# Exchanging the order in which ScalarE and VectorE read the first two finished PSUM banks of a pair

## The chip, the core and the metric

One core of a Trainium2 chip runs the whole program. The metric is device microseconds (us) of one launch. The engines are TensorE (PE in the profile, with its weight loads as PEld), VectorE (DVE), ScalarE (ACT), GpSimd (POOL) and SyncE (SP, which issues transfers).

## The reference

Attention within chunks of 64 tokens makes `x`, and a two-layer network with softplus between the layers makes the output. All data is fp32.

```python
scores = scale * q_c @ k_c.T                 # 8 batches x 8 heads x 9 chunks of 64 x 64, head size 64
attn = exp(scores - max) / (sum + 1e-09)
x = (attn @ v_c) as 4608 tokens x 512
h = x @ w_in                                 # w_in 512 x 2048
g = max(h, 0) + log1p(exp(-abs(h)))          # softplus
out = g @ w_out                              # w_out 2048 x 512
```

## The kernel before

**Tiling.** The 4608 tokens are nine blocks of 512 (`MT`). Each operand of a matmul is split into a high and a low fp32r image, and three matmuls (high by high, low by high, high by low) make one product. Blocks 0 to 2 are computed plainly: first layer (line 635), softplus on ScalarE (line 652), second layer (line 1002). Blocks 3 to 8 are computed in three "supers" of two blocks each (blocks 3 and 4, 5 and 6, 7 and 8). A super runs over eight "pairs", and a pair is two neighbouring column blocks of `w_in`. Pairs are named by super and number, `0_0` to `2_7`, 24 in all.

**A pair.** Its first layer is a 2x2 block product made of seven products of sums (as in Strassen's and Winograd's schemes) instead of eight. They accumulate in four PSUM banks, and two bank pairs are allocated as two tiles named `pa`, from a pool of two (lines 778 to 789). Tile A holds banks 1 and 2, tile B holds banks 0 and 3. TensorE computes P1 (bank 1), P2 (bank 2), P0 (bank 0), P3 (bank 3), then P4 on top of bank 1, P5 on top of bank 2 and P6 on top of bank 0. With P5 the banks of tile A are final, and the next pair's P1 needs tile A to have been read to the end.

What ScalarE, VectorE and GpSimd do with the banks:

- `hold` (lines 791 and 792, ScalarE) copies banks 0, 1 and 2 after P0, P1 and P2 into SBUF (`wib` in the profile, from the tile `wib3`).
- `mix` (lines 794 to 805) makes six sums. `d` and `c22` read SBUF alone and run on GpSimd. `e` reads bank 3, `f` adds bank 1 to `d`, `f2` subtracts bank 2 from `f` in place, and `c11` adds bank 0 to that; these four run on VectorE. In the profile `f` is the group `wib<-pa,wib` of line 805; `e`, `f2` and `c11` are `wib<-wib,pa`.
- `soft` (lines 811 to 817, ScalarE) makes the four softplus blocks of the pair: `soft10` of bank 1, `soft01` of bank 2, `soft11` of the result of `c22`, `soft00` of the result of `c11`. In the profile these are `ends<-pa` and `ends<-wib` of line 816 in supers 0 and 1, and `qe<-pa`, `eT<-pa`, `wo_hi<-pa` and the like of line 814 in super 2 (`BOTH`), whose results stay in SBUF.
- `sp_hi` and `sp_lo` split the softplus blocks into images (`g_hi` on ScalarE, `g_lo` on VectorE: lines 656 and 660, in super 2 lines 918 and 922).

The four steps that read tile A when it is final are `soft10`, `soft01`, `f` and `f2`. `soft10` and `f` read bank 1, `soft01` and `f2` read bank 2.

**What else runs there.** In supers 0 and 1, `soft01` and `soft11` write a tile that `spill_store` (line 820, SP) sends to memory, and `soft01` of the next pair waits until it has landed. In between the pairs lie "bursts" of attention for later blocks. They use `pa` tiles, VectorE transposes (line 544, `eT<-qe`) and ScalarE's exp (line 583). The exp needs another activation table, so the first softplus behind a burst has an `ACT_TABLE_LOAD` ahead of it. In super 2 the second layer is also computed with sums of products (lines 895, 922 and 938), and GpSimd and ScalarE prepare its weights (lines 863 to 881).

**What sets the order.** All work is written down as tasks with an engine, a cost, an urgency (`urg`) and the tasks that it needs (`Plan`, lines 34 to 157). A list scheduler goes through simulated time, gives each free engine the most urgent task that is ready by its own cost figures, and emits the instructions in that order. The tile framework then adds the semaphore waits, by tile and not by bank. A task that is ready later in the simulated time can therefore fall behind other tasks of its engine, and each engine runs its instructions in the order in which they were emitted. TensorE's own order is fixed ahead of that by hand-written lists. The pair's tasks are added in lines 1417 to 1480.

Of the kernel before, what the change touches and what calls it, by code (L numbers as in the profile page):

```python
# [160 lines left out]
def chunked_attention_softplus_ffn(  # L161
# [972 lines left out]
    def due(g):  # L1134
        if isinstance(g, tuple):
            n, second, j = g
            if n in BOTH:
                return D0 + SUPER * n + (98 + 1.36 * j if second else 12.2 * j + 9)
            return D0 + SUPER * n + (8 * PAIR + 2.6 * j if second else PAIR * j + 9)
        return T0 + TG * g  # L1140

    def tag(at):
        return "_".join(map(str, at)) if isinstance(at, tuple) else at
# [4 lines left out]
    for u, (g, is_in, fc) in enumerate(units):  # L1148
        (of_in if is_in else of_out)[fc] = u
        d = due(g) - 4  # L1150
# [30 lines left out]
    for i in range(FIRST_BLK):  # L1181
        d, kw = ATT_AT[i], KS
# [115 lines left out]
    for key, (pv, ps) in bursts.items():  # L1298
        d, at = due(key), tag(key)
        for n in range(2):  # L1300
            needs, rel = [], []
            if pv is not None:
                i = 2 * pv + n
# [12 lines left out]
            if ps is not None:  # L1316
                i = 2 * ps + n
# [21 lines left out]
        for n in range(2):  # L1339
            i = a + n  # L1340
# [24 lines left out]
    for j in range(FC // 2):  # L1365
        d = due(FC + 3 * j)
# [23 lines left out]
    for n, m in enumerate(SUPERS):  # L1390
        d = due((n, 0, 0)) - X_URG
        x_in = [f"xh{TPM * m + t}" for t in range(2 * TPM)]
        for k in range(7):
# [6 lines left out]
            needs = x_in + gone  # L1400
            if k in X_SUMS:
# [8 lines left out]
                needs = [f"xs{n}_{k}"] + gone  # L1410
            if k == 1:
                needs = needs + [f"xH{n}_0"]
# [4 lines left out]
    for at, w in enumerate(pairs):  # L1417
        n, j, name = w["s"], w["j"], w["name"]
        d = due((n, 0, j)) - 9
        for part in range(2):  # L1420
            needs = [] if at > 1 else [f"G1_{FAST * FC - 1}"]
            if not at and not part:
                needs = [f"B{BURST_AT[-1]}_{i}" for i in range(2)]
            if n == 0:
                needs += [f"wd{j}_{i}" for i in range(3)] + own
            if n in BOTH and j % 2:
                needs += [f"x{q}{n}_{k}" for q in "HL" for k in range(7)]
            plan.add(f"ring{part}_{name}", QUEUE["ring"], ISSUE[QUEUE["ring"]], partial(ring_load, w, part), needs, urg=d - 20, kb=660 if part else 880,
                     take=[(("ring", "other")[n in BOTH and j % 2] + str(part), [f"P{6 if part else 3}_{name}"])] if at or part else [],
                     after=[f"ring{part}_{pairs[at - 1]['name']}"] if at else [])  # L1430
        for k in range(7):
            needs = [f"ring{k // NX}_{name}", f"xH{n}_{k}", f"xL{n}_{k}"]
            needs += [before[f"P{k}_{name}"]] + {4: [f"s1_{name}"], 5: [f"s2_{name}"], 6: [f"s0_{name}", f"e_{name}"]}.get(k, [])
            take = []
            if k == ORDER[0]:
                take = [("pa", [f"soft10_{name}", f"soft01_{name}", f"f2_{name}"])]
            elif k == ORDER[2]:
                take = [("pa", [f"c11_{name}", f"e_{name}"])]
            plan.add(f"P{k}_{name}", "PE", PM, partial(product, w, k), needs, urg=1e6, take=take)
        for q in range(3):  # L1440
            past = [f"{t}_{pairs[at - 1]['name']}" for t in (("soft11",), ("c22", "f"), ("d",))[q]] if at else []
            plan.add(f"s{q}_{name}", "ACT", 0.59, partial(hold, w, q), [f"P{q}_{name}"] + past, urg=-3 if n in BOTH else -2)
        for what, needs in (
            ("d", ["s1", "s2"]), ("e", ["s0", "P3"]), ("c22", ["e", "d"]), ("f", ["d", "P5"]), ("f2", ["f", "P5"]),
            ("c11", ["f2", "P6"]),
        ):
            pool = what in MIX_POOL
            past = [f"soft00_{pairs[at - 1]['name']}"] if at and what == "f" else []
            plan.add(f"{what}_{name}", "POOL" if pool else "DVE", 1.3 if pool else 0.69, partial(mix, w, what),
                     [f"{t}_{name}" for t in needs] + past, urg=-2)  # L1450
        a, b = (v_["name"] for v_ in w["first"])
        for i, jj, what in ((1, 0, "P5"), (0, 1, "P5"), (1, 1, "c22"), (0, 0, "c11")):
            kept = [f"lo{v_['name']}" for v_ in w["second"]] if j == FC // 2 - 1 else [f"us{name}"]
            take = {(1, 0): [("uu0", [f"lo{a}", f"lo{b}"])], (0, 1): [("uu1", kept)]}.get((i, jj), [])
            needs = [f"{what}_{name}"] + {(0, 0): [f"soft10_{name}"], (1, 1): [f"soft01_{name}"]}.get((i, jj), [])
            if n in BOTH:
                take = []
                if j > 1:
                    needs += [f"R{i}_{j - 2}", f"vt{j - 2}_{i}"] + [f"own{j - 2}{q}" for q in range(2)] * i
                elif j:  # L1460
                    needs += [f"B{tag(list(bursts)[-1])}_{b}" for b in range(2)]
                else:
                    needs += [f"lo{v_['name']}" for w_ in pairs[at - FC // 2 : at] for v_ in w_["second"]]
            plan.add(f"soft{i}{jj}_{name}", "ACT", 0.6, partial(soft, w, i, jj), needs, urg=-2, table="softplus", take=take)
        if n in BOTH:
            continue
        if j < FC // 2 - 1:
            plan.add(f"us{name}", QUEUE["us"], ISSUE[QUEUE["us"]], partial(spill_store, w), [f"soft01_{name}", f"soft11_{name}"], urg=-1, kb=400)
            a, b = (v_["name"] for v_ in w["second"])
            plan.add(f"ul{name}", QUEUE["ul"], ISSUE[QUEUE["ul"]], partial(spill_load, w), [f"us{name}", f"soft{1 - j % 2}{j % 2}_{n}_{FC // 2 - 1}"],  # L1470
                     urg=due((n, 1, 2 * j + 2)) - 12, kb=400,
                     take=[(f"uu{j % 2}", [f"lo{a}", f"lo{b}"])], after=[f"ul{n}_{j - 1}"] if j else [])
        for group in ("first", "second"):
            for i in (1, 0) if group == "first" else (0, 1):
                v_ = w[group][i]
                b = v_["name"]
                src = f"ul{name}" if group == "second" and j < FC // 2 - 1 else f"soft{i}{int(group == 'second')}_{name}"
                plan.add(f"hi{b}", "ACT", 0.62, partial(sp_hi, v_), [src], urg=-1, take=[("g", [f"G2_{b}"])],
                         after=[f"hi{w[group][1]['name']}"] if group == "first" and i == 0 else [])
                plan.add(f"lo{b}", "DVE", 0.69, partial(sp_lo, v_, False), [f"hi{b}"], urg=-1)  # L1480
# [198 lines left out]
```

## Time and profile before

| what | value |
|---|---|
| time, median of 3 runs | 832.38 us (832.22 to 832.39) |
| the profiled execution's own time | 831.0 us |
| its span in the trace | 829.2 us |
| mean granted TensorE clock | 0.994 |
| idle time of TensorE ahead of line 786, put down to VectorE line 805 | 4.4 us in 6 waits |
| the same, put down to ScalarE line 816 | 2.6 us in 5 waits |
| the same, put down to ScalarE line 814 | 0.5 us in 1 wait |

A row of a timeline in the profile gives the start in us, the duration in us, engine, line, operation, `out<-in` by the program's names, shape, and how many instructions were taken together (x8: eight in a row; the duration is then that of all). In square brackets stands the idle time just before on this engine and what ended it. A row of the waits says which engine and line waited for which, then us in total, times, and the longest. TensorE's waits show at its weight loads (PEld), which come just before their matmuls.

### The profile page before, as it was taken

To read this page: it belongs to the slowest core of one execution; us is meant where nothing else is said; L and a number is where in the kernel's file an instruction comes from. 1 tells how busy PE (TensorE), PEld (TensorE's weight loads), DVE (VectorE), ACT (ScalarE), POOL (GpSimd) and SP (SyncE) were. 2 spreads that over 40 slices of the span, in tenths; PEclk is the share of its full clock that TensorE was granted. 3 is DMA by queue.
4 is the path that set the end of the run, shared out by engine and by line. 5 is a ranking of instruction groups with operands and counts; after the bars stand their busy time and mean duration, and the time that the engine had idled before them with its cause. 6 is when DMAs were issued, how large, how long until landed. Compare 5 with 4: busy or idle time off the path is not lost.

```text
span 829.2 us, 15528 instructions
## 1 busy us (share of the span) xinstructions
PE 809.3 (98%) x5675; PEld 664.0 (80%) x5675; DVE 583.3 (70%) x938; ACT 403.1 (49%) x664; POOL 406.9 (49%) x467
## 2 busy tenths in 40 slices
PE   8799999999999999999999999999999999999997
PEld 7688778888887888888888888888887787878886
DVE  4898987087478777667487888483878935555984
ACT  3767764345344564344434434434454644454551
POOL 1457659879975822322334212132188539972213
PEclk9899999999999999999999999999999999999999
DMA  9977758644674454776749536859558565666563
GB/s 207 251 181 201 188 174 238 199 111 123 152 199 112 112 145 153 226 214 180 205 164 225 151 105 205 230 162 233 158 149 269 190 228 187 208 218 212 158 208 68
DMA packets 202877, 151.27 MB, mean 182 GB/s; under 512 B 161136, under 2 KB 176752, under 8 KB 198576
## 3 DMA queue, kind: packets, MB, share of 16 engines
q1 hardware_dynamic: 189424, 99.66, 44.6%
q0 software_dynamic: 11232, 50.34, 19.8%
q8 instruction: 45, 0.74, 0.4%
q10 hardware_dynamic: 2144, 0.26, 0.2%
q14 instruction: 32, 0.26, 0.1%
HBM read 106.95 MB, written 41.94 MB: 180 GB/s over the span
## 4 chain that ended last, share of the span: by engine, by line
PE 74%; DVE 8%; DMA 5%; ACT 4%; POOL 3%; issue 3%; SPq 2%; DVEq 0%; POOLq 0%; ACTq 0%
PE po L1002 29%; PE pa L786 22%; PE pa L644 13%; PE po L938 8%; PE pa L608 2%; DVE wib L805 2%; PE pa L520 1%; DMA raw<-in_moe_w_in_dram 1%; DVE g_lo L660 1%; SPq L359 1%; POOL raw L873 1%; DMA images<-raw 1%; POOL wib L805 1%; DVE eT L544 1%; ACT ends L816 1%
## 5 line engine op out<-in xcount | busy, mean ns | idle before, releaser
L805 POOL TENSOR_TENSOR wib<-wib 128x512 f32<-128x512 f32 x48 | 65.5, 1364 | 180.7 <-ACT wib L792 158.5
L1002 PE MATMUL po<-late,g_hi 128*128 128x512 f32 x420 | 128.8, 392 | 0.0
L786 PE MATMUL pa<-wi_hi,xb 128*128 128x512 f32 x304 | 94.8, 393 | 1.8 <-DVE wib L805 1.1
L544 DVE STREAM_TRANSPOSE eT<-qe 32x256 f32<-32x256 f32 x216 | 93.9, 435 | 3.1
L1002 PEld LDWEIGHTS po<-late,g_hi 128*128 128x128 f32 x420 | 78.2, 188 | 16.6 <-DVE raw L1009 0.2
L1002 PE MATMUL po<-wo_hi,g_hi 128*128 128x512 f32 x224 | 85.2, 396 | 0.0
L786 PE MATMUL pa<-wib,xb 128*128 128x512 f32 x360 | 84.9, 389 | 0.0
L1002 PE MATMUL po<-wo_hi,g_lo 128*128 128x512 f32 x224 | 84.2, 392 | 0.6 <-DVE g_lo L660 0.6
L1002 PE MATMUL po<-wo_lo,g_hi 128*128 128x512 f32 x224 | 84.2, 392 | 0.0
L1002 PE MATMUL po<-late,g_lo 128*128 128x512 f32 x224 | 83.5, 390 | 0.3 <-DVE g_lo L660 0.3
L786 PEld LDWEIGHTS pa<-wib,xb 128*128 128x128 f32 x360 | 67.6, 188 | 14.1
L805 DVE TENSOR_TENSOR wib<-wib,pa 128x512 f32<-128x512 f32 x72 | 49.3, 685 | 36.6 <-ACT wib L792 21.9
L652 ACT ACTIVATE u<-pa 128x512 f32<-128x512 f32 (+1 forms) x50 | 29.0, 581 | 93.5 <-PE pa L644 91.6
L792 ACT COPY wib<-pa 128x512 f32<-128x512 f32 x72 | 40.5, 587 | 61.5 <-PE pa L786 61.5
L786 PEld LDWEIGHTS pa<-wi_hi,xb 128*128 128x128 f32 x304 | 56.5, 188 | 16.6 <-ACT ends L816 2.6
L660 DVE TENSOR_TENSOR g_lo<-ends,g_hi 128x512 fp32r<-128x512 f32 x64 | 49.4, 778 | 22.5 <-ACT g_hi L656 21.9
L656 ACT CAST g_hi<-ends 128x512 fp32r<-128x512 f32 x64 | 39.1, 618 | 46.4 <-PE po L1002 42.6
L786 PE MATMUL pa<-wi_lo,xb 128*128 128x512 f32 x152 | 59.2, 390 | 0.0
L746 POOL DMA_DIRECT2D xb<-scratch x39 | 22.1, 567 | 67.7 <-PE pa L786 52.4
L660 DVE TENSOR_TENSOR g_lo<-u,g_hi 128x512 fp32r<-128x512 f32 (+1 forms) x32 | 31.2, 976 | 30.0 <-ACT g_hi L656 24.3
L1002 PEld LDWEIGHTS po<-wo_hi,g_lo 128*128 128x128 f32 x224 | 42.4, 189 | 10.1 <-DVE g_lo L660 1.2
L805 DVE TENSOR_TENSOR wib<-pa,wib 128x512 f32<-128x512 f32 x24 | 16.6, 690 | 47.7 <-ACT ends L816 21.1
(288 smaller groups left out, 1831.0 us busy)
## 6 DMA issues: line engine op xcount, KB each, us to landing
xb<-scratch POOLq DMA_DIRECT2D x19, 1024.0 KB, 6.0
xb<-scratch POOLq DMA_DIRECT2D x20, 768.0 KB, 5.5
raw<-in_moe_w_in_dram SPq DMA_DIRECT2D x16, 512.0 KB, 5.3
raw<-in_moe_w_out_dram SPq DMA_DIRECT2D x16, 512.0 KB, 4.9
scratch<-ends SPq DMA_DIRECT2D x16, 512.0 KB, 3.1
out_dram<-raw SPq DMA_DIRECT2D x28, 256.0 KB, 4.0
spill<-ends SPq DMA_DIRECT2D x14, 512.0 KB, 3.9
ends<-spill SPq DMA_DIRECT2D x14, 512.0 KB, 4.1
```

Of the source, the lines that this page charges most:

```text
L544: nc.vector.transpose(live["eT", i][d : d + BL, tb], e[s : s + BL, kb])
L608: nc.tensor.matmul(pa[o, a, col : col + C], vt[r, 4 * j + 2 * h2 + c2, :], eT[r, :, 4 * c2 + 2 * j + h2, :], start=True, stop=True,)
L644: nc.tensor.matmul(ph, wt[:, c, :], x[:, ts_, c, :], start=(n == 0), stop=(n == 3 * KC - 1))
L652: nc.scalar.activation(w["u"], w["ph"], AF.Softplus)
L656: nc.scalar.copy(w["hi"], w["u"])
L660: (nc.gpsimd if pool else nc.vector).tensor_tensor(w["lo"], w["u"], w["hi"].bitcast(F32), op=ALU.subtract)
L746: on("ring").dma_start(t[:, : cols.stop - cols.start], src[:, cols])
L786: nc.tensor.matmul(w["bank"][BANK[k]], wts[:, q, c, :], x[:, c, :], start=k < NX and c + n == 0, stop=c == 1 and n == 2, skip_group_check= ...
L792: nc.scalar.copy(tmp_of(n), w["bank"][n])
L805: (nc.gpsimd if what in MIX_POOL else nc.vector).tensor_tensor(out, a, b, op=op)
L938: nc.tensor.matmul(live["acc", ACC[k]][ct][:, cols], (w[:, q] if k > 1 else w[q])[:, ct * P : (ct + 1) * P], g[:, cols], start=k < 3 and j ...
L1002: nc.tensor.matmul(pos[w["m"]][t], terms[n][0][:, j * P : (j + 1) * P], terms[n][1], start=(w["first"] and n == 0), stop=n == 2 and (w["la ...
```

## The change

`f2` now needs `soft01` besides `f`, and no longer names P5. The four softplus tasks are added in another order: `soft01` first (it needs P5), then `soft10`, which now needs `f` and `soft01` instead of P5. `soft11` needs `soft10` where it needed `soft01`. So in the planner `soft01` (bank 2) can stand beside `f` (bank 1), and after them `soft10` (bank 1) beside `f2` (bank 2).

```diff
@@ -1441,7 +1441,7 @@
             past = [f"{t}_{pairs[at - 1]['name']}" for t in (("soft11",), ("c22", "f"), ("d",))[q]] if at else []
             plan.add(f"s{q}_{name}", "ACT", 0.59, partial(hold, w, q), [f"P{q}_{name}"] + past, urg=-3 if n in BOTH else -2)
         for what, needs in (
-            ("d", ["s1", "s2"]), ("e", ["s0", "P3"]), ("c22", ["e", "d"]), ("f", ["d", "P5"]), ("f2", ["f", "P5"]),
+            ("d", ["s1", "s2"]), ("e", ["s0", "P3"]), ("c22", ["e", "d"]), ("f", ["d", "P5"]), ("f2", ["f", "soft01"]),
             ("c11", ["f2", "P6"]),
         ):
             pool = what in MIX_POOL
@@ -1449,10 +1449,10 @@
             plan.add(f"{what}_{name}", "POOL" if pool else "DVE", 1.3 if pool else 0.69, partial(mix, w, what),
                      [f"{t}_{name}" for t in needs] + past, urg=-2)
         a, b = (v_["name"] for v_ in w["first"])
-        for i, jj, what in ((1, 0, "P5"), (0, 1, "P5"), (1, 1, "c22"), (0, 0, "c11")):
+        for i, jj, what in ((0, 1, "P5"), (1, 0, "f"), (1, 1, "c22"), (0, 0, "c11")):
             kept = [f"lo{v_['name']}" for v_ in w["second"]] if j == FC // 2 - 1 else [f"us{name}"]
             take = {(1, 0): [("uu0", [f"lo{a}", f"lo{b}"])], (0, 1): [("uu1", kept)]}.get((i, jj), [])
-            needs = [f"{what}_{name}"] + {(0, 0): [f"soft10_{name}"], (1, 1): [f"soft01_{name}"]}.get((i, jj), [])
+            needs = [f"{what}_{name}"] + {(0, 0): [f"soft10_{name}"], (1, 1): [f"soft10_{name}"], (1, 0): [f"soft01_{name}"]}.get((i, jj), [])
             if n in BOTH:
                 take = []
                 if j > 1:
```

TensorE's instructions and their order are the same in both kernels. On the other engines the planner's answer moves. The first place is VectorE in pair `0_3`, the first pair behind a burst. The rows of line 805 are, in order, `f`, `f2` and `c11`; `L544` are transposes of the burst. Before:

```order
L544 STREAM_TRANSPOSE eT<-qe 32x256 [waits DVE_49]
L544 STREAM_TRANSPOSE eT<-qe 32x256 x3
L805 TENSOR_TENSOR wib_3768<-pa,wib_3768 128x512 [waits Activation_49,Pool_49]
L805 TENSOR_TENSOR wib_3768<-wib_3768,pa 128x512 [waits DVE_49]
L805 TENSOR_TENSOR wib_3768<-wib_3768,pa 128x512 [waits DVE_49,PE_49]
L544 STREAM_TRANSPOSE eT<-qe 32x256 x4
L660 TENSOR_TENSOR g_lo<-ends,g_hi 128x512 [waits Activation_49]
```

And in the changed kernel:

```order
L544 STREAM_TRANSPOSE eT<-qe 32x256 [waits DVE_49]
L544 STREAM_TRANSPOSE eT<-qe 32x256 x3
L805 TENSOR_TENSOR wib_3768<-pa,wib_3768 128x512 [waits Activation_49,Pool_49]
L544 STREAM_TRANSPOSE eT<-qe 32x256 x4
L805 TENSOR_TENSOR wib_3768<-wib_3768,pa 128x512 [waits Activation_49]
L805 TENSOR_TENSOR wib_3768<-wib_3768,pa 128x512 [waits DVE_49,PE_49]
L660 TENSOR_TENSOR g_lo<-ends,g_hi 128x512 [waits Activation_49]
```

Four transposes that stood behind `c11` now stand between `f` and `f2`. Pairs `0_6`, `1_0`, `1_3` and `1_6` have the same four transposes between `f` and `f2`; no other pair has anything there, before or now. `f` waits for ScalarE (`Activation_49`) in both kernels: before for `soft10`, now for `soft01`. `f2` now waits here for `soft10`.

The second place is ScalarE in the same pair, from the last `hold` on. Before (the two rows `ends<-pa` are `soft10` and `soft01`, the two `ends<-wib` are `soft00` and `soft11`):

```order
L792 COPY wib_3768<-pa 128x512 [waits PE_49]
L816 ACT_TABLE_LOAD [waits PE_49]
L816 ACTIVATE ends<-pa 128x512 [waits Activation_49]
L816 ACTIVATE ends<-pa 128x512 [waits DMAHW1_49,DVE_49]
L816 ACTIVATE ends<-wib_3768 128x512 [waits DVE_49,Activation_49]
L816 ACTIVATE ends<-wib_3768 128x512 [waits Pool_49]
```

And in the changed kernel, where `ends<-pa` are `soft01` and `soft10`, and `ends<-wib` are `soft11` and, behind a cast, `soft00`:

```order
L792 COPY wib_3768<-pa 128x512 [waits PE_49]
L816 ACT_TABLE_LOAD [waits DMAHW1_49]
L816 ACTIVATE ends<-pa 128x512 [waits PE_49]
L816 ACTIVATE ends<-pa 128x512 [waits DVE_49]
L816 ACTIVATE ends<-wib_3768 128x512 [waits Pool_49]
L656 CAST g_hi<-ends 128x512 [waits Activation_49]
L816 ACTIVATE ends<-wib_3768 128x512 [waits DVE_49]
```

The wait for TensorE has moved from the table load to the softplus behind it. The load itself now waits for the spill's transfer (`DMAHW1_49`), which belongs to `soft01`, the first softplus now. The second softplus waits for VectorE, here for `f`; in pairs without transposes between `f` and `f2` it waits for `f2`.

The third place is VectorE between pairs `2_1` and `2_2` in super 2. The rows of line 805 here are `e`, `f` and `f2` of `2_2`. Before:

```order
L922 TENSOR_TENSOR g_lo<-eT,g_hi 128x512 [waits PE_49,Activation_49]
L895 TENSOR_TENSOR eT<-eT 128x512 [waits DVE_49]
L895 TENSOR_TENSOR eT<-qe,eT 128x512 [waits DVE_49]
L805 TENSOR_TENSOR wib_3768<-wib_3768,pa 128x512 [waits Activation_49]
L805 TENSOR_TENSOR wib_3768<-pa,wib_3768 128x512 [waits Activation_49,Pool_49]
L805 TENSOR_TENSOR wib_3768<-wib_3768,pa 128x512 [waits Activation_49]
```

And in the changed kernel:

```order
L805 TENSOR_TENSOR wib_3768<-wib_3768,pa 128x512 [waits Activation_49]
L922 TENSOR_TENSOR g_lo<-eT,g_hi 128x512 [waits Activation_49]
L895 TENSOR_TENSOR eT<-eT 128x512 [waits DVE_49]
L895 TENSOR_TENSOR eT<-qe,eT 128x512 [waits DVE_49]
L805 TENSOR_TENSOR wib_3768<-pa,wib_3768 128x512 [waits Activation_49,Pool_49]
L805 TENSOR_TENSOR wib_3768<-wib_3768,pa 128x512 [waits DVE_49]
```

The split of the previous pair's last softplus block (`g_lo`) and the two sums of line 895 have moved from ahead of `e` to a place between `e` and `f`, because the cast that they need (line 918) moved behind ScalarE's work at the start of `2_2`. On GpSimd the order is the same apart from buffer numbers, and SP's order hardly differs.

## The prediction

> **What bounds the kernel now.** I read the page first, then TensorE's waits, then the timeline around the places where TensorE waits for readers of tile A.
>
> ```profile
> span 829.2 us, 15528 instructions
> PE 809.3 (98%) x5675; PEld 664.0 (80%) x5675; DVE 583.3 (70%) x938; ACT 403.1 (49%) x664; POOL 406.9 (49%) x467
> PEld pa L786 <- DVE wib L805: 4.4, 6, 1.5
> PEld pa L786 <- ACT ends L816: 2.6, 5, 0.5
> PEld pa L786 <- ACT ends L814: 0.5, 1, 0.5
> ```
>
> TensorE is busy for 98% of the span and its work is not touched, so the change can move the time only through TensorE's idle time. The last three rows (the third from super 2 alone) are all of it that hangs on the four steps: 7.5 us in 12 of 24 pairs, under 1% of the time. That is the most the change could give back. What it could cost is set by the other 12 pairs, where tile A is free early enough, and by how much later it may come free.
>
> Pair `0_2` shows how the four steps run, without anything in their way:
>
> ```profile
> 353.15 0.60 ACT L816 ACTIVATE ends<-pa 128x512 f32<-128x512 f32 x1 [2.13 <-PE pa L786]
> 353.86 0.69 DVE L805 TENSOR_TENSOR wib<-pa,wib 128x512 f32<-128x512 f32 x1 [2.11 <-ACT ends L816]
> 354.58 0.60 ACT L816 ACTIVATE ends<-pa 128x512 f32<-128x512 f32 x1 [0.83 <-DVE wib L805]
> 355.21 1.48 DVE L805 TENSOR_TENSOR wib<-wib,pa 128x512 f32<-128x512 f32 x2 [0.66 <-ACT ends L816]
> ```
>
> P5 ends just before 353.15. Then come `soft10` (0.60), `f` (0.69), `soft01` (0.60) and `f2` (0.69, with `c11` behind it in the same row), each 0.03 to 0.11 us after the end of the one before: 2.75 us to 355.90. `soft01` reads bank 2 and `f` bank 1, yet `soft01` starts 0.03 us after `f` has ended, and the row names VectorE as what it waited for. So readers of one tile already follow one another here, whether they share a bank or not.
>
> **Part 1: the chain itself, 0 us.** In the changed kernel's order rows `f` still waits for ScalarE, now for `soft01`, and the second softplus waits for VectorE. They read different banks, but the wait goes by tile. The chain becomes `soft01`, `f`, `f2`, `soft10`: the same four durations, 2.58 us, plus hand-overs. One hand-over between engines becomes one within VectorE; `f2` and `c11` behind it show that at (1.48 - 2 x 0.69) = 0.1, no more than the 0.03 to 0.11 between engines. I take 0 and bound it at 0.05 us to either side in each of the six pairs of super 2 whose P1 waits on this chain, of which `2_1` is one:
>
> ```profile
> 687.03 0.60 ACT L814 ACTIVATE qe<-pa 128x512 f32<-128x512 f32 x1 [3.49 <-PE pa L786]
> 689.83 0.30 PEld L786 LDWEIGHTS pa<-wi_hi,xb 128*128 128x128 f32 x2 [0.54 <-DVE wib L805]
> ```
>
> From the first softplus to the next P1 it is 2.80 us, of which TensorE waits 0.54. With the same length these waits stay: 0 us, bounds -0.3 to +0.3. Pairs of supers 0 and 1 that don't wait have TensorE work of the second layer in between, and an unchanged length leaves them unchanged.
>
> **Part 2: five pairs behind a burst, +4.0 us.** Pair `0_3`, before:
>
> ```profile
> 371.18 3.56 DVE L544 STREAM_TRANSPOSE eT<-qe 32x256 f32<-32x256 f32 x8
> 373.13 1.28 ACT L816 ACT_TABLE_LOAD   x1 [4.90 <-PE pa L786]
> 374.43 0.60 ACT L816 ACTIVATE ends<-pa 128x512 f32<-128x512 f32 x1
> 375.13 0.69 DVE L805 TENSOR_TENSOR wib<-pa,wib 128x512 f32<-128x512 f32 x1 [0.40 <-ACT ends L816]
> 375.85 1.48 DVE L805 TENSOR_TENSOR wib<-wib,pa 128x512 f32<-128x512 f32 x2
> 376.57 0.60 ACT L816 ACTIVATE ends<-pa 128x512 f32<-128x512 f32 x1 [1.55 <-DVE wib L805]
> 376.52 0.19 PEld L1002 LDWEIGHTS po<-wo_hi,g_lo 128*128 128x128 f32 x1
> 377.22 0.30 PEld L786 LDWEIGHTS pa<-wi_hi,xb 128*128 128x128 f32 x2 [0.52 <-ACT ends L816]
> 377.36 1.79 DVE L544 STREAM_TRANSPOSE eT<-qe 32x256 f32<-32x256 f32 x4
> ```
>
> The table load waits for P5 and stands 1.28 us on the path; TensorE could go on at 377.22 - 0.52 = 376.70 and waits until 377.22. In the changed kernel the load waits for the spill's transfer alone. ScalarE is idle for 4.90 us ahead of 373.13, so the load is over before P5 and `soft01` runs from 373.13 to 373.73. That would let `f` start 1.3 us sooner, but VectorE is in the eight transposes until 371.18 + 3.56 = 374.74: `f` runs from 374.77 to 375.46, a gain of 0.36. Then come the four transposes that now stand ahead of `f2`: 1.79 us in the last row, which end at 377.25. `soft10`, which waits for `f`, runs beside them and ends at about 376.1, so `f2` waits for nothing else and runs from 377.28 to 377.97. `f2` is the last reader; with the 0.05 us that stand between the end of `soft01` (377.17) and TensorE, P1 of the next pair starts at 378.02, 0.80 later than before.
>
> So P1 comes 3.28 us after the end of the transposes that run when P5 ends. The other four pairs have the same two groups in the same place:
>
> ```profile
> 418.70 3.56 DVE L544 STREAM_TRANSPOSE eT<-qe 32x256 f32<-32x256 f32 x8
> 424.74 0.30 PEld L786 LDWEIGHTS pa<-wi_hi,xb 128*128 128x128 f32 x2 [0.52 <-ACT ends L816]
> 498.89 1.73 DVE L544 STREAM_TRANSPOSE eT<-qe 32x256 f32<-32x256 f32 x4
> 503.08 0.30 PEld L786 LDWEIGHTS pa<-wi_hi,xb 128*128 128x128 f32 x2 [0.51 <-ACT ends L816]
> 544.60 3.56 DVE L544 STREAM_TRANSPOSE eT<-qe 32x256 f32<-32x256 f32 x8
> 550.64 0.30 PEld L786 LDWEIGHTS pa<-wi_hi,xb 128*128 128x128 f32 x2 [0.52 <-ACT ends L816]
> 592.12 3.56 DVE L544 STREAM_TRANSPOSE eT<-qe 32x256 f32<-32x256 f32 x8
> 598.17 0.30 PEld L786 LDWEIGHTS pa<-wi_hi,xb 128*128 128x128 f32 x2 [0.52 <-ACT ends L816]
> ```
>
> `0_6`: 422.26 + 3.28 = 425.54 against 424.74, +0.80. `1_0`: 500.62 + 3.28 = 503.90 against 503.08, +0.82. `1_3`: 551.44 against 550.64, +0.80. `1_6`: 598.96 against 598.17, +0.79. Together with `0_3`, +4.01 us. TensorE's work behind each place follows in a fixed order, so the delays add up. `c11` is late too, by about 1.4 us, but the bank that it frees is wanted two products after P1, so nothing waits for it.
>
> **Part 3: the pair `2_0`, -0.52 us.** It has the table load without the transposes:
>
> ```profile
> 673.09 1.28 ACT L814 ACT_TABLE_LOAD   x1 [4.90 <-PE pa L786]
> 675.80 1.48 DVE L805 TENSOR_TENSOR wib<-wib,pa 128x512 f32<-128x512 f32 x2
> 677.18 0.30 PEld L786 LDWEIGHTS pa<-wi_hi,xa 128*128 128x128 f32 x2 [0.52 <-ACT ends L814]
> ```
>
> With the load hidden in the 4.90 us, the chain of 2.80 us starts at 673.09 and tile A is free at 675.89; TensorE wants it at 677.18 - 0.52 = 676.66. The whole wait goes, and the next thing that is late is TensorE itself.
>
> **Part 4: what else moves, 0 us.** `soft01`, now first, waits for the spill of the pair before. The latest of these against its pair is in `0_2`:
>
> ```profile
> 346.02 0.77 SPq L820 DMA_DIRECT2D spill<-ends  x1
> DMA to landing us min/median/max: 2.6/3.9/7.3
> ```
>
> By the median it lands at 349.9, 3.2 us ahead of 353.15; by the longest of all at 353.3, 0.2 us late, and an unstalled pair has more slack than that. 0 us.
>
> In `2_2`, `g_lo` and two sums of line 895 now stand between `e` and `f`:
>
> ```profile
> 693.07 1.11 DVE L895 TENSOR_TENSOR eT<-eT 128x512 f32<-128x512 f32 x1
> 696.09 0.72 ACT L877 CAST raw<-raw 128x256 fp32r<-128x256 f32 x2
> 696.23 0.69 DVE L805 TENSOR_TENSOR wib<-wib,pa 128x512 f32<-128x512 f32 x1 [1.32 <-ACT wib L792]
> 700.39 0.69 DVE L805 TENSOR_TENSOR wib<-pa,wib 128x512 f32<-128x512 f32 x1 [3.48 <-ACT wo_hi L814]
> ```
>
> Between the end of `e` (696.92) and `f` there are 3.48 us. Three operations of 0.69 (the price of the rows of line 805 beside them) take 2.1, and of 1.11 take 3.3; the cast that they need stands on ScalarE behind the two of line 877, which end at 696.81, so by 0.6 us for itself it ends about 0.5 us after `e`. So `f` is 0 to 0.4 us late, up to 0.5 with hand-overs. I take 0, since two of the three are likely short, and keep +0.5 for the range.
>
> Against that, a delay could vanish where TensorE waits for something that doesn't move with it. The one such place is `2_5`:
>
> ```profile
> 738.54 0.41 ACT L877 CAST raw<-raw 128x256 fp32r<-128x256 f32 x1 [2.88 <-POOL raw L873]
> 741.64 0.30 PEld L786 LDWEIGHTS pa<-wi_hi,xb 128*128 128x128 f32 x2 [1.48 <-DVE wib L805]
> ```
>
> Here GpSimd holds a cast that stands ahead of the softplus, which makes the wait 1.48 - 0.54 = 0.94 longer than in `2_1`. If GpSimd's chain kept its time, up to 0.94 of the delay would vanish. But its `d` and `c22` wait for ScalarE's `hold` in each pair and so for TensorE: the whole chain shifts along. I take 0 and keep -0.94.
>
> **The sum.** 0 + 4.01 - 0.52 + 0 = +3.49 us. The profiled execution's 831.0 becomes 834.5, its span of 829.2 becomes 832.7. The median of the runs stands 1.38 above the profiled execution, so it goes from 832.38 to 835.9. About 0.2% (1.7 us) is what a measurement of this kernel can tell from no change.
>
> **The rivals.**
>
> *The reads overlap after all.* If `f` ran beside `soft01` and `f2` beside `soft10`, the chain would be shorter by the two softplus steps (1.2 us), the six waits of 0.54 in super 2 would go (-3.24), part 2 would stay (the transposes hold `f2` in any case) and so would part 3: +4.01 - 0.52 - 3.24 = +0.25, 832.6 us, no change to be seen. Against it stand the row at 354.58 and the waits in the order rows. The Trainium skill ("PSUM — Partial Sum Buffer", "Specifications (TRN2)") says that ScalarE and VectorE can access PSUM in parallel at full bandwidth as long as no bank collides. By that rule alone this rival would be the forecast; the trace neither confirms nor denies it, since the semaphores keep the reads apart before the memory could. Chance 0.06.
>
> *The hidden table load wins (the other side).* If `f2` came right behind `soft10` with no transposes ahead, it would run from 376.12 to 376.81 in `0_3`, and TensorE would wait 0.16 instead of 0.52. Five times -0.36 and part 3 make -2.3 us: 830.1. It decides between two and three transposes: `f2` is as late as before when it ends at 377.17, which leaves 376.48 - 375.46 = 1.02 us behind `f`, and four take 1.79. Against it stand the order rows, which put all four ahead of `f2`. For it would be a VectorE that gets to the first eight sooner. Chance 0.05.
>
> *More knock-on.* `2_2` costs its 0.5, and the later casts of the first softplus blocks hold up a second-layer matmul by as much once: 836.9. TensorE did wait for such images in this run, so a new wait can't be excluded:
>
> ```profile
> PEld po L1002 <- DVE g_lo L660: 1.9, 3, 1.0
> ```
>
> But these are only three waits in the whole span. Chance 0.08.
>
> **How the numbers follow.** The forecast has 0.79, the rivals 0.06, 0.05 and 0.08, and 0.02 are left for delays swallowed to within 0.2%. The range leaves out the first two rivals: below, 835.9 - 0.94 - 0.3 (hand-overs) - 0.4 (the medians' spread, and five costs worked out from rows of two decimals) = 834.2; above, 835.9 + 0.5 + 0.3 + 0.4 = 837.1. Faster 0.05; same 0.06 + 0.02 = 0.08; slower 0.87.
>
> **What would show it.** Right: TensorE's five waits ahead of line 786 behind a burst are about 1.3 us each and are put down to VectorE's line 805; the table loads of line 816 stand ahead of P5's end; four transposes stand between two rows of line 805; `2_0` has no wait; the six of super 2 stay at 0.5, now put down to ScalarE. Wrong: two rows of tile A's readers that overlap in time, or waits behind the bursts under 0.6.

## The result

The changed kernel is slower: 835.91 us, the median of 8 runs (834.35 to 838.73). Before takes 831.66 in 8 runs (827.13 to 832.39; the five later ones were faster than the three that the prediction saw). The ratio is 1.0068, 95% interval 1.0050 to 1.0086, or +4.2 to +7.2 us. The +3.5 us of the prediction lies below that. That the median came out at its 835.9 to the digit is luck: it stands on a median before that was 0.7 us lower (831.66 against 832.38).

The spans of the two profiled executions are 829.2 and 832.4 us. They understate the change. From the start to P1 of pair `0_0` both kernels run the same instructions, and this stretch took 317.15 us before and 314.51 after; in the experiments it took 313.95 to 319.75. The granted clock goes with it: the five profiled executions with a mean clock of 0.994 or 0.995 took 315.71 to 319.75 us here, the five with 0.997 or 0.998 took 313.95 to 315.94. From there to the end, where the clock is 1.00 in both kernels, it is 512.05 against 517.89, **+5.84 us**. So I compare the rest from here on, pair by pair: a pair's time is from the start of TensorE's first weight load of its P1 to that of the next pair, read from PEld's rows of line 786. These repeat to 0.06 us for pairs in which nothing was changed, such as `0_0` to `0_2` in all ten kernels. Times here are read from rows of two decimals, so a difference can be off by 0.01 or 0.02.

The page and TensorE's waits of the changed kernel:

```profile
span 832.4 us, 15500 instructions
PE 808.0 (97%) x5675; PEld 662.0 (80%) x5675; DVE 581.5 (70%) x938; ACT 402.1 (48%) x664; POOL 407.1 (49%) x467
...
PEld pa L786 <- DVE wib L805: 6.8, 5, 1.4
PEld pa L786 <- ACT wo_hi L814: 4.8, 4, 1.5
...
PEld pa L786 <- ACT qe L814: 0.5, 1, 0.5
PEld pa L786 <- ACT late L814: 0.5, 1, 0.5
```

The waits on the readers of tile A rose from 7.5 to 12.6 us: five of about 1.35 behind the bursts (0.52 before), six in super 2, none behind `2_0`. That is 5.2 of the 5.84 us.

**Pair `0_3`**, the rows of the chain out of the timeline of all engines: it is the chain that the prediction wrote down, 2.7 us earlier on the time axis (P1 at 375.35 instead of 378.02).

```profile
365.55 1.28 ACT L816 ACT_TABLE_LOAD   x1
370.38 0.60 ACT L816 ACTIVATE ends<-pa 128x512 f32<-128x512 f32 x1 [3.55 <-PE pa L786]
368.47 3.56 DVE L544 STREAM_TRANSPOSE eT<-qe 32x256 f32<-32x256 f32 x8
372.06 0.69 DVE L805 TENSOR_TENSOR wib<-pa,wib 128x512 f32<-128x512 f32 x1
372.78 1.79 DVE L544 STREAM_TRANSPOSE eT<-qe 32x256 f32<-32x256 f32 x4
372.79 0.60 ACT L816 ACTIVATE ends<-pa 128x512 f32<-128x512 f32 x1 [1.80 <-DVE wib L805]
374.61 1.48 DVE L805 TENSOR_TENSOR wib<-wib,pa 128x512 f32<-128x512 f32 x2
375.35 0.30 PEld L786 LDWEIGHTS pa<-wi_hi,xb 128*128 128x128 f32 x2 [1.35 <-DVE wib L805]
```

The table load is over at 366.83, 3.5 us before P5. `soft01` ends at 370.98, but `f` starts only when the eight transposes end at 372.03. `f2` has everything that it needs at 373.39, when `soft10` ends, and stands behind the four transposes until 374.61.

**Pair `2_2`** is where the prediction went wrong. On VectorE the rows are `e`, the split of `2_1`'s last block, the two sums of line 895, and `f`; ahead of the split is its cast on ScalarE:

```profile
697.60 0.69 DVE L805 TENSOR_TENSOR wib<-wib,pa 128x512 f32<-128x512 f32 x1 [4.24 <-ACT wib L792]
698.07 0.62 ACT L918 CAST g_hi<-eT 128x512 fp32r<-128x512 f32 x1
698.73 1.54 DVE L922 TENSOR_TENSOR g_lo<-eT,g_hi 128x512 fp32r<-128x512 f32 x1 [0.44 <-ACT g_hi L918]
700.31 1.11 DVE L895 TENSOR_TENSOR eT<-eT 128x512 f32<-128x512 f32 x1
701.45 1.11 DVE L895 TENSOR_TENSOR eT<-qe,eT 128x512 f32<-128x512 f32 x1
702.49 0.68 DVE L805 TENSOR_TENSOR wib<-pa,wib 128x512 f32<-128x512 f32 x1
704.57 0.30 PEld L786 LDWEIGHTS pa<-wi_hi,xa 128*128 128x128 f32 x2 [1.31 <-ACT wo_hi L814]
```

The three operations took 1.54, 1.11 and 1.11 us, 3.76 together; the prediction had taken two of them at 0.69, which is what the last of them took in the kernel before (at 694.21). `f` is 0.77 late, and so is P1: 1.31 of wait instead of 0.54.

**Pair `2_4`** was not in the prediction at all. Here the same late cast acts by way of GpSimd:

```profile
720.82 0.62 ACT L918 CAST g_hi<-wo_hi 128x512 fp32r<-128x512 f32 x1
721.48 0.69 DVE L922 TENSOR_TENSOR g_lo<-wo_hi,g_hi 128x512 fp32r<-128x512 f32 x1 [0.80 <-ACT g_hi L918]
722.20 1.66 DVE L895 TENSOR_TENSOR wo_hi<-wo_lo,wo_hi 128x512 f32<-128x512 f32 x1
723.90 1.11 DVE L895 TENSOR_TENSOR wo_lo<-wo_lo,wo_lo 128x512 f32<-128x512 f32 x1
724.93 0.68 DVE L805 TENSOR_TENSOR wib<-wib,pa 128x512 f32<-128x512 f32 x1
725.76 1.28 POOL L805 TENSOR_TENSOR wib<-wib 128x512 f32<-128x512 f32 x1 [0.79 <-DVE wib L805]
727.01 0.73 POOL L873 TENSOR_TENSOR raw<-raw 128x256 f32<-128x256 f32 x1
727.78 0.41 ACT L877 CAST raw<-raw 128x256 fp32r<-128x256 f32 x1 [2.87 <-POOL raw L873]
728.09 0.59 ACT L814 ACTIVATE wo_lo<-pa 128x512 f32<-128x512 f32 x1
730.88 0.30 PEld L786 LDWEIGHTS pa<-wi_hi,xa 128*128 128x128 f32 x2 [1.48 <-ACT wo_hi L814]
```

The rows are one chain: cast, split, two sums, `e` (late), `c22` on GpSimd (which waits 0.79 for `e`), GpSimd's own sum of line 873, its cast on ScalarE (line 877), and behind that cast the pair's first softplus. It starts 10.85 us after the pair's P1 at 717.24; before, it was 10.09 after a P1 at 715.14:

```profile
725.23 0.59 ACT L814 ACTIVATE wo_hi<-pa 128x512 f32<-128x512 f32 x1
```

### The profile page after: what moved, and what is told of

It is laid out like the page before. It is cut to its first block, busy times and chain, and to the rows that moved or that the text cites. A ratio compares the mean times of both kernels' runs of the same rounds, so it can differ in the third digit from the quotient of the medians.

```text
span 832.4 us, 15500 instructions
## 1 busy us (share of the span) xinstructions
PE 808.0 (97%) x5675; PEld 662.0 (80%) x5675; DVE 581.5 (70%) x938; ACT 402.1 (48%) x664; POOL 407.1 (49%) x467
## 4 chain that ended last, share of the span: by engine, by line
PE 80%; DVE 11%; ACT 3%; SPq 2%; DMA 2%; issue 1%; POOL 1%; DVEq 0%; POOLq 0%; ACTq 0%
PE po L1002 31%; PE pa L786 23%; PE pa L644 15%; PE po L938 8%; DVE eT L544 3%; DVE wib L805 2%; SPq L359 2%; PE pa L608 2%; PE pa L520 2%; DVE qe L595 1%; DVE g_lo L660 1%; DMA raw<-in_moe_w_out_dram 1%; DMA raw<-in_moe_w_in_dram 1%; ACT wib L792 0%; DVE qe L507 0%
## 5 line engine op out<-in xcount | busy, mean ns | idle before, releaser
L544 DVE STREAM_TRANSPOSE eT<-qe 32x256 f32<-32x256 f32 x216 | 93.9, 435 | 3.1
L816 ACT ACTIVATE ends<-pa 128x512 f32<-128x512 f32 x32 | 19.2, 598 | 77.9 <-PE pa L786 51.2
```

The lines of the kernel that those rows point to most:

```text
L544: nc.vector.transpose(live["eT", i][d : d + BL, tb], e[s : s + BL, kb])
L816: nc.scalar.activation(u_tiles(j)[i], src, AF.Softplus)
```

## The experiments

**Theories.** Mine: behind the bursts the four transposes between `f` and `f2` are the cost, and they are there because the planner charges the table's load to `soft01`; in super 2 the cost is the cast of the previous pair's last block, which falls behind the next pair's first steps; and the reads don't overlap because of waits by tile, while the memory would let them. The rivals: not the transposes but `soft10` as last reader makes P1 late; GpSimd's own chain sets `2_2` and `2_4`; the reads of two engines hold each other up.

The pairs that answer, in us (the rest is from P1 of `0_0` to the end):

| kernel | `0_3` | `2_0` | `2_2` | `2_4` | `1_7` | rest | ratio to before (95%) |
|---|---|---|---|---|---|---|---|
| before | 15.43 | 15.44 | 12.66 | 12.88 | 63.57 | 512.05 | |
| changed | 16.27 | 14.96 | 13.43 | 13.64 | 63.73 | 517.89 | 1.0068 (1.0050 to 1.0086) |
| e1 supers 0, 1 only | 16.27 | 15.44 | 12.65 | 13.19 | 63.60 | 516.55 | 1.0058 (1.0040 to 1.0075) |
| e2 super 2 only | 15.44 | 14.96 | 13.42 | 13.95 | 63.32 | 513.50 | 1.0021 (1.0004 to 1.0038) |
| e3 table not counted | 15.14 | 14.97 | 13.42 | 13.61 | 64.98 | 513.67 | 1.0021 (1.0006 to 1.0037) |
| e4 urgent casts | 16.26 | 14.98 | 12.65 | 13.03 | 63.62 | 515.59 | 1.0056 (1.0040 to 1.0072) |
| e5 changed, banks apart | 16.28 | 14.96 | 12.97 | 12.96 | 63.56 | 514.26 | 1.0019 (1.0006 to 1.0032) |
| e6 before, banks apart | 15.72 | 15.44 | 12.24 | 13.68 | 64.29 | 511.43 | 0.9988 (0.9975 to 1.0002) |
| e7 f2 early, urgent casts | 15.14 | 14.97 | 12.65 | 12.67 | 64.85 | 511.45 | 0.9983 (0.9967 to 0.9999) |
| e8 e7 with banks apart | 14.96 | 14.96 | 12.24 | 12.24 | 64.81 | 507.36 | 0.9936 (0.9918 to 0.9955) |

### e1 and e2: the two halves

e1 makes the change for supers 0 and 1 alone; e2 for super 2 alone, by the same edit with `n in BOTH`. In e1:

```diff
-            ("d", ["s1", "s2"]), ("e", ["s0", "P3"]), ("c22", ["e", "d"]), ("f", ["d", "P5"]), ("f2", ["f", "soft01"]),
+            ("d", ["s1", "s2"]), ("e", ["s0", "P3"]), ("c22", ["e", "d"]), ("f", ["d", "P5"]), ("f2", ["f", "soft01" if n not in BOTH else "P5"]),
...
-        for i, jj, what in ((0, 1, "P5"), (1, 0, "f"), (1, 1, "c22"), (0, 0, "c11")):
+        for i, jj, what in ((0, 1, "P5"), (1, 0, "f"), (1, 1, "c22"), (0, 0, "c11")) if n not in BOTH else ((1, 0, "P5"), (0, 1, "P5"), (1, 1, "c22"), (0, 0, "c11")):
```

The needs of the softplus tasks go by the same condition.

> The change in supers 0 and 1 alone; super 2 as before. The time of a pair is from its P1 to the next pair's P1. Theory (the four transposes between f and f2 make P1 late behind a burst; late casts make 2_2 and 2_4 late): the pairs 0_3, 0_6, 1_0, 1_3, 1_6 take 16.3 us as in the changed kernel (15.43 before), 2_0 keeps 15.44, 2_2 keeps 12.66, 2_4 keeps 12.88; together about +4.3 us to before. Rival (the exchange makes super 2's loss through what supers 0 and 1 leave behind): 2_2 and 2_4 take 13.4 and 13.6 here too.

> The change in super 2 alone; supers 0 and 1 as before. Theory: the five pairs behind a burst keep 15.43 us; 2_0 falls from 15.44 to 14.96, 2_2 rises to 13.4, 2_4 to 13.6, the end by up to 0.4: about +1.4 us to before. Rival as for the other half: 2_2 and 2_4 keep their times, -0.5 us.

Measured: the rest is +4.50 us in e1 and +1.45 in e2, together 5.95 against 5.84 for the whole change. e1's five pairs behind a burst take 16.27 to 16.29 and its `2_2` is untouched; e2's five keep 15.44, and its `2_0`, `2_2` and `2_4` move as in the changed kernel. So the halves are independent and the rival falls. One reading is off: `2_4` is 0.3 longer than forecast in both (13.19, 13.95). The first softplus starts there when it did in the whole kernels (10.04 us after P1 in e1, 10.81 in e2), but the row of `f` names GpSimd's sum of line 873 as what released it, 0.45 us behind the end of that softplus; in the kernel before and in the changed one `f` followed the softplus after 0.10. So GpSimd moves this place by some tenths from kernel to kernel.

### e3: the same needs, without the transposes

```diff
-            plan.add(f"soft{i}{jj}_{name}", "ACT", 0.6, partial(soft, w, i, jj), needs, urg=-2, table="softplus", take=take)
+            plan.add(f"soft{i}{jj}_{name}", "ACT", 0.6, partial(soft, w, i, jj), needs, urg=-2, table=None if i + jj == 1 else "softplus", take=take)
```

The planner then thinks that `soft01` ends with `f`, and `f2` follows at once.

> The change in full, but the planner does not count the activation table's load for the two softplus steps on the PSUM banks; f2 and c11 then follow f and no transposes stand between. ScalarE's steps are in the changed order. Theory: P1 behind a burst waits 0.1 to 0.2 us instead of 1.35, and the five pairs take 15.1 us (15.43 before, 16.27 changed): about -5.9 us to the changed kernel, super 2 unchanged from it. Rival (not the transposes but soft10, now last behind soft01 and f, makes P1 late): the waits stay near 1.3 and the pairs at 16.2.

The timeline at `0_3` in e3, with VectorE's rows from `f` on, `soft01` and `soft10`, and TensorE:

```profile
371.70 0.60 ACT L816 ACTIVATE ends<-pa 128x512 f32<-128x512 f32 x1 [3.55 <-PE pa L786]
373.38 0.69 DVE L805 TENSOR_TENSOR wib<-pa,wib 128x512 f32<-128x512 f32 x1
374.11 1.48 DVE L805 TENSOR_TENSOR wib<-wib,pa 128x512 f32<-128x512 f32 x2
374.89 0.60 ACT L816 ACTIVATE ends<-pa 128x512 f32<-128x512 f32 x1 [2.59 <-DVE wib L805]
375.54 0.30 PEld L786 LDWEIGHTS pa<-wi_hi,xb 128*128 128x128 f32 x2 [0.22 <-ACT ends L816]
```

`soft10` is still the last reader, and TensorE waits 0.22 instead of 1.35. The five pairs take 15.14 to 15.16, 1.13 less each. That settles it for the transposes, and for the planner's table cost as what put them there. The total missed: 4.2 us less than the changed kernel, not 5.9, because the end of super 1 (`1_7`) took 1.25 more and `0_7` 0.38 more. Inside each of these two pairs TensorE now waits 0.52 for VectorE's `e` (line 805), where it did not wait before. And in `1_7` it waits for VectorE's splits (line 660), 1.0 more in e3 than in the changed kernel, whose row stands second:

```profile
PEld po L1002 <- DVE g_lo L660: 3.2, 8, 1.3
```

```profile
PEld po L1002 <- DVE g_lo L660: 2.2, 5, 1.3
```

Part of what the pairs give is taken back where VectorE is behind.

### e4: the late casts

```diff
-                plan.add(f"ghi{k}_{j}", "ACT", 0.62, partial(g_hi, k, j), src + free, urg=d - 3 if soon else -2.5,
+                plan.add(f"ghi{k}_{j}", "ACT", 0.62, partial(g_hi, k, j), src + free, urg=d - 3 if soon and k > 1 else -2.5,
...
-                plan.add(f"glo{k}_{j}", "POOL" if pool else "DVE", 1.3 if pool else 0.69, partial(g_lo, k, j), [f"ghi{k}_{j}"], urg=d - 2 if soon else -2.5)
+                plan.add(f"glo{k}_{j}", "POOL" if pool else "DVE", 1.3 if pool else 0.69, partial(g_lo, k, j), [f"ghi{k}_{j}"], urg=d - 2 if soon and k > 1 else -2.5)
```

> The change in full, but in super 2 the casts and splits of a pair's softplus blocks (lines 918 and 922, for the products R0 and R1) are urgent, so that they and the two sums of line 895 stand ahead of the next pair's e again. Theory: 2_2 goes from 13.43 to about 12.7 us and 2_4 from 13.64 to about 12.9, the five pairs behind a burst stay at 16.3: about -1.5 us to the changed kernel. Rival (GpSimd's own chain of lines 863 to 881 sets both pairs): 2_2 may improve, 2_4 stays at 13.6.

TensorE at the P1 behind `2_2` and behind `2_4` in e4:

```profile
704.97 0.30 PEld L786 LDWEIGHTS pa<-wi_hi,xa 128*128 128x128 f32 x2 [0.54 <-ACT wo_hi L814]
...
730.65 0.30 PEld L786 LDWEIGHTS pa<-wi_hi,xa 128*128 128x128 f32 x2 [0.89 <-ACT wo_hi L814]
```

`2_2` is back at 12.65 and `2_4` at 13.03 (13.43 and 13.64 in the changed kernel), `2_5` falls from 13.59 to 12.84 as well (below the 13.61 of the kernel before, so this is a gain of its own and nothing that the change had lost), and the five pairs behind the bursts stay at 16.27. The rest is 2.3 us shorter than the changed kernel's (1.5 expected). So what `2_4` had lost was not set by GpSimd's own chain, which had been started late. What is left of its wait, 0.89, hangs on GpSimd all the same: the first softplus starts 9.88 us after P1, earlier than before, but `f` is released by the sum of line 873 0.45 us after it ends.

### e5 and e6: readers of different banks apart

Both take the framework's waits between readers of different banks out; readers of one bank still wait for each other. `mix` and `soft` call `apart` with each instruction. e5 is the changed kernel, e6 the kernel before. Their lines are shifted: 805 is 820, 814 is 830, 816 is 832.

```diff
+    READS = {"soft10": 1, "f": 1, "soft01": 2, "f2": 2}
+
+    def apart(w, what, ins):
...
+        for other, was in done.items():
+            if READS[other] != READS[what]:
+                if (what, other) != ("f2", "f") and other[:4] != what[:4]:
+                    tc.declare_no_dep(ins.ins, was.ins, reason="reads of two banks")
+            else:
+                tc.add_manual_dep(ins.ins, was.ins.name, sync, reason="reads of one bank")
```

> The changed kernel with the waits between readers of different banks of tile A taken out (soft01 and f, soft10 and f2; readers of one bank still wait for each other). Theory (the framework's waits by tile keep the reads apart, the memory would not): f and soft01 overlap, f2 and soft10 overlap, each still 0.6 to 0.7 us; the 0.54 waits of super 2 go (pairs of about 12.1 us), those of 2_2, 2_4 and 2_5 shrink by 0.6 to 1.4; the five pairs behind a burst stay at 16.3, since f2 is behind the transposes there. About -5 us to the changed kernel. Rival (reads of two engines hold each other up in PSUM): softplus or sums get longer where they overlap, and super 2 keeps 12.65.

> The kernel before with the waits between readers of different banks taken out, its order kept. Theory: where its order is soft10, f beside soft01, f2, the chain falls from 2.8 to 2.0 us, and super 2's waits of 0.54 go and those of 0.73 and 1.48 fall by 0.7; behind a burst its order is soft10, f, f2, soft01, which share a bank each with the next, so the six waits of 0.52 stay. About -3.5 us to before. Rival: as for the other, no change.

ScalarE's `soft10` and `soft01` and VectorE's `f` in pair `2_2` of e6:

```profile
700.00 0.60 ACT L830 ACTIVATE wo_hi<-pa 128x512 f32<-128x512 f32 x1 [2.88 <-PE pa L786]
700.49 0.60 ACT L830 ACTIVATE wo_lo<-pa 128x512 f32<-128x512 f32 x1
700.70 0.69 DVE L820 TENSOR_TENSOR wib<-pa,wib 128x512 f32<-128x512 f32 x1 [3.47 <-ACT wo_hi L830]
```

`soft01` reads bank 2 from 700.49 to 701.09 and `f` reads bank 1 from 700.70 to 701.39, each as long as alone. TensorE's wait behind `2_2`, 0.54 before, is gone. In e5 super 2 fell by 0.5 in `2_1`, `2_2`, `2_3` and `2_6` and by 0.7 in `2_4`, but `2_5` fell by 0.2 only, where 0.6 to 1.4 were expected. P1 behind the burst in `0_3` waits as long as ever, with `f2` behind the transposes, as expected:

```profile
374.22 0.69 DVE L820 TENSOR_TENSOR wib<-pa,wib 128x512 f32<-128x512 f32 x1
374.94 1.79 DVE L544 STREAM_TRANSPOSE eT<-qe 32x256 f32<-32x256 f32 x4
376.77 1.48 DVE L820 TENSOR_TENSOR wib<-wib,pa 128x512 f32<-128x512 f32 x2
377.52 0.30 PEld L786 LDWEIGHTS pa<-wi_hi,xb 128*128 128x128 f32 x2 [1.37 <-ACT g_hi L656]
```

The row names ScalarE's line 656, but VectorE's `f2` ends at 377.46, right ahead. e5's rest is 3.6 us below the changed kernel's (5 expected). e6 gave 0.6 of the 3.5 expected: `2_1`, `2_2`, `2_3` and `2_6` are 0.4 to 0.5 shorter each and `2_5` 0.3, but `2_4` is 0.8 longer, `1_7` 0.7 and `0_3` 0.3. In `2_4` the end of the changed kernel's chain is seen again: VectorE's two splits ahead of `e` take 4.93 us together (3.56 before) and the two sums 1.67 and 1.12 (0.69 and 1.67 before), `c22` waits 0.79 for the late `e`, and the first softplus starts 11.45 us after P1 instead of 10.09. In `1_7` TensorE waits 2.8 us for VectorE's splits (line 660) where it waited 1.9. What makes these splits and sums slower or later was not tested, and the 0.3 has no cause here.

### e7 and e8: the parts that were left, put right

e7 is the changed kernel with `("f2", ["f", "P5"])` again, so that the planner sets `f2` behind `f`, and with e4's casts. e8 is e7 with the banks apart.

> The changed kernel with f2 again needing P5 and not soft01, and with the casts of super 2 urgent. Theory: no transposes between f and f2, pairs behind a burst 15.15 us, 2_0 14.97, 2_2 12.65, 2_4 about 13.0: about -1.9 us to before, less what the end of super 1 may take (1.4 in the run without the table's cost). Rival (soft10 last is what costs): 16.3 behind the bursts.

> All three together: f2 early, casts urgent, waits between different banks taken out. Theory: f is done before or right after P5, P1 behind a burst does not wait (pairs of 14.9 us), super 2's pairs take about 12.1 us and 2_5 loses up to 1.4 of its wait: -6 to -7.4 us to before. Rival (reads hold each other up): about as e7.

In e7 P1 behind `0_3` waits as in e3, again with `soft10` last:

```profile
379.47 0.30 PEld L786 LDWEIGHTS pa<-wi_hi,xb 128*128 128x128 f32 x2 [0.22 <-ACT ends L816]
```

It is 0.6 us below before in the rest: the pairs gave what was expected, and `1_7` took 1.3 back of the 1.4 that was allowed for; `0_7` took 0.4, which was not. In e8 the timeline at `0_3` (`soft01`, `f`, `f2` with `c11`, `soft10`, P1):

```profile
371.81 0.60 ACT L832 ACTIVATE ends<-pa 128x512 f32<-128x512 f32 x1 [3.55 <-PE pa L786]
373.49 0.69 DVE L820 TENSOR_TENSOR wib<-pa,wib 128x512 f32<-128x512 f32 x1
374.28 0.60 ACT L832 ACTIVATE ends<-pa 128x512 f32<-128x512 f32 x1 [1.86 <-DVE wib L820]
374.29 1.48 DVE L820 TENSOR_TENSOR wib<-wib,pa 128x512 f32<-128x512 f32 x2
375.47 0.41 PEld L786 LDWEIGHTS pa<-wi_hi,xb 128*128 128x128 f32 x2
```

`soft10` and `f2` start within 0.01 us of each other and TensorE no longer waits. In `2_1`, where no transposes are near:

```profile
683.79 0.69 DVE L820 TENSOR_TENSOR wib<-pa,wib 128x512 f32<-128x512 f32 x1 [0.66 <-PE pa L786]
685.08 0.60 ACT L830 ACTIVATE eT<-pa 128x512 f32<-128x512 f32 x1 [3.49 <-PE pa L786]
685.57 0.59 ACT L830 ACTIVATE qe<-pa 128x512 f32<-128x512 f32 x1
685.71 1.48 DVE L820 TENSOR_TENSOR wib<-wib,pa 128x512 f32<-128x512 f32 x2 [1.23 <-ACT eT L830]
```

`f` no longer waits for `soft01`, so it runs when bank 1 is final, while TensorE still works on P5 in bank 2; behind P5 only two steps in a row are left, `soft01` and then `soft10` and `f2` side by side. Pairs `2_1` to `2_6` take 12.24 us each, none of the twelve P1 waits any more (two waits of 0.7 for `e` have come up inside `0_7` and `1_7`, and `1_7` is 1.2 longer than before), and the rest is 4.7 us below before. e8 is faster than both kernels, by 0.6% against the kernel before: the change with what it lacked.

## Why the prediction was right or wrong

- **What bounds the kernel**: right. TensorE's work stayed the same and the waits on tile A carried the change. But the cost did not fall where the prediction looked for it, in the 12 pairs whose next P1 did not wait: all waits for tile A that grew are behind pairs that had waited already.
- **Part 1, the chain at 0**: right. In `2_1`, which nothing disturbed, TensorE still waits 0.54, now for ScalarE. The pair took 0.08 more. The reason given, waits by tile, was shown by e5 and e6.
- **Part 2, five pairs, +4.01**: right in mechanism and size. They measured +0.83 to +0.85 each, 4.2 together: `f2` starts 0.04 behind the transposes where 0.03 was taken, and so on at each step. e3 showed that it was the transposes.
- **Part 3, `2_0`, -0.52**: right, -0.48.
- **Part 4, `2_2` at 0: this step failed.** "I take 0, since two of the three are likely short": all three were long (1.54, 1.11, 1.11), and a row of 1.11 for one of them stood in the prediction. The cast was where the prediction put it, 0.4 us behind `e`; the three operations were not 2.1 to 3.3 us long but 3.76. GpSimd was busy beside all three, from 698.44 to 703.16. The term measured +0.77, more than the 0.5 kept for the range. So the sign "the six of super 2 stay at 0.5" failed here and in `2_4`.
- **Part 4, what else moves: a term was missing.** The late cast also stands ahead of `2_4`'s `e`, and the delay goes on through GpSimd and the cast of line 877: +0.76. The prediction had that chain in hand for `2_5`, but asked only whether it could swallow a delay, not whether it could start later. e4 showed both terms to be the casts' place: all of `2_2`'s and 0.6 of `2_4`'s 0.76. The last +0.4 is at the end of super 2 (`2_7`: 74.9 before, 75.3 changed, 75.2 in e2, 74.9 in e1) and belongs to super 2's half. There TensorE's rows of line 938 have two new waits for ScalarE, 0.18 for a cast of line 918 and 0.29 for a copy of line 951; neither is in the kernel before or in e1. What makes these two late was not tested.
- **The sum**: 3.49 against 5.84 in the profiled executions. 1.53 of the 2.35 between them are `2_2` and `2_4`, 0.4 the end, 0.2 the five pairs, and 0.2 to 0.3 other pairs.
- **The rivals.** "The reads overlap after all" did not happen in the changed kernel. Its price of 3.24 counted 0.54 for six waits, but two of these were 0.73 and 1.48; e5, where the reads overlap, lay 3.6 us below the changed kernel. And what the Trainium skill says ("PSUM — Partial Sum Buffer", "Specifications (TRN2)"), that ScalarE and VectorE can access PSUM in parallel at full bandwidth as long as no bank collides, agrees with e6 and e8: the softplus steps took 0.59 to 0.60 us and the sums 0.69 side by side, as alone. "The hidden table load wins" is what e3 and e7 made true, with waits of 0.22 where 0.16 was worked out. "More knock-on" named the right place with too small a price.

## What to carry to other kernels

Before you plan for two engines to read different banks at once, look at what the waits are drawn on: here the exchange brought no overlap, because the waits went by the two-bank tile. When a step in a planned order gets a new need, read the order for what slips into the gap on every engine, and follow each slipped operation to the next engine that waits for it. Price VectorE's work by the rows that lie beside busy GpSimd, if GpSimd will be busy there.

## What was not expected

- VectorE's sums of 128x512 that read SBUF alone took 0.69 us where GpSimd stood idle for most of the time (721.48 in `2_4`) and 1.11 to 1.66 where a GpSimd sum was already running (700.31, 722.20). Where VectorE's sum had started first it could keep its time: at 694.21 before it took 0.69, and the GpSimd sum that started 0.13 us after it took 1.71, against 1.28 for the one at 725.76. `f`, which also reads PSUM, kept 0.68 in the middle of them (702.49). Three sums of line 881 in `2_2` show what GpSimd paid, first in the changed kernel and then before, where VectorE was idle for most of them:

```profile
699.69 3.47 POOL L881 TENSOR_TENSOR raw<-raw 128x256 f32<-128x256 f32 x3
```

```profile
698.54 2.11 POOL L881 TENSOR_TENSOR raw<-raw 128x256 f32<-128x256 f32 x3
```

The Trainium skill ("SBUF — State Buffer", "Who interferes with whom") states the rule behind it: a VectorE instruction with two SBUF inputs contends with a GpSimd instruction that reads SBUF, and one with at most one SBUF input (outside the two-port modes) does not. These rows agree: `f`, with one SBUF input, kept 0.68.
- The first 314 to 320 us, the same instructions in every kernel here, differed by up to 5.8 us between profiled executions, as much as the whole change. Medians of a few runs can hide or make an effect of this size; times of single pairs repeat to some hundredths.
- Where a bank is done early, its reader can run beside TensorE's work on the other bank of the same tile: `f` in e8 took its usual 0.69 us during P5.
